# Attention, routed experts and a rational MLP on one core: decay rows, first transfers, gates and the attention order changed

## The chip, the core and the metric

The kernel runs on one core of a Trainium2 chip. Five engines work side by side, each through its own list of instructions in order: TensorE (PE, its weight loads shown as PEld), VectorE (DVE), ScalarE (ACT), GpSimd (POOL) and SyncE (SP, which here only issues transfers). They wait for each other and for transfers by semaphores. The metric is device time in microseconds (us), less is better.

## The reference

Three stages, in fp32. Attention with a decay, per batch b (4) and head h (8), S = 576, D = 64:

```python
scores = q @ k.T / sqrt(D);  cum = cumsum(log(clip(f, 1e-4, 1)))
scores = where(causal, -1e9, scores + cum[:, None] - cum[None, :])
attn = softmax(scores);  x = attn @ v          # x: (2304, 512) after the heads are joined
```

Experts (8, one per token), on the 2304 tokens:

```python
logits = x @ w_gate;  e = argmax(logits);  gate_w = softmax(logits)[e]
eom = sigmoid((x @ w_output_gate)[e])
out = gate_w * eom * (relu(x @ w1[e]) @ w2[e])  # w1: 512x1024, w2: 1024x512
```

Then a dense pair 512 to 2048 to 512 with g = P(h)/Q(h) between, a cubic over a quadratic in |h|.

The gate of a token, gate_w * eom, is a positive number, so it may be put on the token's row of x ahead of the expert or on the expert's output.

## The kernel before, in words

**Attention.** Work goes by pairs of heads: 16 pairs, four to a batch. A pair's scores are made in seven steps of 128 query rows (L456 and its neighbours: one product with the high parts of k and q, kh and qs, and one with kl and q2s). kl holds the low part of k and, in two more rows, the pair's decay (high and low part), q2s a copy of q and two rows of ones, so that one product adds the low part and the decay. DVE takes the row minimum (L478, L490; the scale is negative), ACT the exponential (L510, L521), PE transposes (L573, L593), DVE or ACT copies the result to SBUF (L290, L292: pT), PE multiplies by v (L616: po), and DVE or ACT copies to ot. The splits into high and low parts are made per half pair: kh (L410) on DVE, qs (L421) on ACT, the low parts and q2s (L415, L424, L429) on POOL, for pair 0 on DVE.

The decay rows come from one chain at the start: load f, clip, log on ACT, a running sum on DVE (L314, scan), its high part (L328) and low part (L332), two stores to DRAM (cum_d), and for every pair a load of two rows for each head into kl (L387).

**Order.** The attention part's order is written by a planner: each operation has a `when` (a priority from constants T_... times the pair's number), a modelled length on each engine that may do it, and the operations and buffers that it needs; of what is ready at about the same time the one with the least `when` goes first, and a copy that two engines could do goes to the one with the earlier modelled end plus DEAR. What comes out is the order on each engine, SP's transfers included.

**Batches.** When the four pairs of a batch are done, DVE inverts the sums (rc, L691), PE and DVE make the logits (L699 to L724), choose (L739 to L744) marks each token's expert in oh, and the gates follow: gates_a on DVE (L750 to L752), gates_x on ACT (L755, L756), gates_b on DVE (L760 to L769), whose last two operations multiply rc by the gate: rg. Then the batch's rows are transposed (L779), scaled by rg (on DVE for batches 0 and 1, L785; copied by ACT and scaled on POOL for 2 and 3) and stored to x_d, five tiles a batch.

**Tail.** After the last pair DVE's order is fixed by hand: choose of batch 3, then a count of the tokens before each token (two matmuls with onesb and after, a scan, cnt, nsl, send, base), interleaved with gates_b; from it a slot of 128 tokens and a place for each token (pos, sidx, pp), one-hot products (so, rs, op_) and a matmul whose result is ids, the token of each place. POOL gathers the rows by ids.

**Experts.** 22 slots: transpose the gathered rows, split into high and low, first matrix (L1169 to L1171), relu, transpose, second matrix, copy (ys, L1193), store to y_d. The expert's weights are split by split_unit (high on ACT, low on DVE, L1037). slot_info makes the list by which weights are loaded. Beside it the dense weights are decoded in pieces (loads from POOL's queue, L1203).

```python
DEAR = {"ACT": 45.9, "DVE": 316.0}      # L37
o_z = plan.op(early, {"DVE": 600}, f_zero, takes=["pr"])
o_f = plan.op(early, {"SP": 1900}, f_load, takes=["t"])
l_c = plan.op(tl + 0.3 * SPAN, {"SP": 1200}, load_c, o_cst, takes=["c"])
for i in range(NI):
    rows_out(i)                          # behind gates_b and the count
nc.scalar.activation(ys, yp.pop(s), AF.Copy)   # L1193
```

Of the kernel before, what the change touches and what calls it, by code (L numbers as in the profile page):

```python
# [21 lines left out]
P = 128  # L22
# [15 lines left out]
DEAR = {"ACT": 45.9, "DVE": 316.0}  # L38

NEAR = 108.2  # L40
# [6 lines left out]
class Op:  # L47
# [90 lines left out]
def tile_attention_moe_mlp(  # L138
# [44 lines left out]
    cum_d = dram.tile([NBH, 2, S], F32, name="cum_d")  # L183
    x_d = dram.tile([NT, DM], F32, name="x_d")
    y_d = dram.tile([NSLOT * P, DM], F32, name="y_d")
# [4 lines left out]
    identf = const.tile([P, P], F32, name="identf")  # L190
    make_identity(nc, identf)

    after = ec.tile([P, P], BF16, name="after")
    nc.gpsimd.memset(after, 1.0)
# [4 lines left out]
    onesb = ec.tile([P, P], BF16, name="onesb")  # L199
    nc.gpsimd.memset(onesb, 1.0)  # L200
# [11 lines left out]
    pref = ec.tile([P, NE], F32, name="pref")  # L212
    nc.gpsimd.iota(pref, pattern=[[-1, NE]], base=NE, channel_multiplier=0, allow_small_or_imprecise_dtypes=True)

    prefs = ec.tile([P, NI, NE], F32, name="prefs")
    nc.gpsimd.tensor_copy(prefs, pref.unsqueeze(1).to_broadcast([P, NI, NE]))
    nc.gpsimd.memset(prefs[TL:, NQ], 0.0)


    with ExitStack() as actx, ExitStack() as rctx:  # L220
# [30 lines left out]
        nc.gpsimd.memset(mask, 0.0)
        nc.gpsimd.memset(mask_t, 0.0)
        for t in [mask[:, (NQ - 1) * P :]] + [mask_t[h * TL : (h + 1) * TL, S // 2 - TL :] for h in range(2)]:
            nc.gpsimd.affine_select(
                out=t, in_=t, compare_op=ALU.is_ge, fill=BIG / SCALE, base=0, pattern=[[-1, t.shape[-1]]], channel_multiplier=1
            )

# [8 lines left out]
        T_STEP = (0.003, 0.167, 0.576, 1.046, 0.372, 0.855, 1.261)  # L266
        T_TRANS = (0.59, 0.851, 0.237, 0.235, -3.102, 0.47, -0.137)
        T_MOVE = (1.284, 1.144, 0.583, -2.797, 0.532, -7.775, 0.103)
        T_LEAST, T_EXP, T_SPLIT, T_SPLIT2 = 0.096, 0.218, 0.342, 0.209
        T_PV, T_PV2, T_OUT = -2.976, 4.84, -4.781  # L270
        T_BATCH, T_BATCHJ, T_ROWS = 0.299, 0.239, -5.772
# [22 lines left out]
        def evac_len(n):  # L294
            return {"ACT": 60 + 0.836 * n, "DVE": 85 + 1.04 * n}

# [29 lines left out]
        def f_high(e):  # L326
            g0["ch"] = wt("pr")[:NBH].bitcast(F32R)
            nc.scalar.activation(g0["ch"], g0["cum"], AF.Copy, scale=1.0 / SCALE)  # L328

        def f_low(e):  # L330
            g0["cl"] = wt("pr")[:NBH].bitcast(F32R)
            nc.vector.scalar_tensor_tensor(  # L332
                g0["cl"], g0["cum"], 1.0 / SCALE, g0["ch"].bitcast(F32), ALU.mult, ALU.subtract
            )

        def f_store(i, t):
            return lambda e: nc.sync.dma_start(out=cum_d[:, i, :], in_=g0[t].bitcast(F32))
# [1172 lines left out]
```

## Time and profile before

| what | value |
|---|---|
| median of 3 runs | 916.08 us (915.52 to 918.97) |
| profiled execution: its own time, its span | 916.76 us, 915.0 us |
| busy share: PE, PEld, DVE, ACT, POOL | 95%, 79%, 81%, 68%, 37% |
| chain that ended last, by engine | PE 41%, DVE 1%, ACT 1% |
| most expensive PE groups | dense layers (L1378 to L1380, L1423 to L1425), experts (L1169 to L1171) |

Shares are means over stages that differ, so the rows below go by stretches: the start to about 30 us, attention to 193, the tail to 220, experts to 500, dense layers to 900. A row of the time order gives start, duration, engine, line, operation, what is written and read, the number merged, and in brackets how long the engine had stood idle and what released it.

### The profile page before, as it was taken

What the parts mean: (1) busy time and instruction counts of PE and PEld (TensorE: products, weight loads), DVE (VectorE), ACT (ScalarE), POOL (GpSimd) and SP (SyncE); (2) the same over time, 40 slices, a digit from 0 to 9 for tenths busy, and PEclk for the clock granted to TensorE, in tenths of its full rate; (3) what the DMA queues carried; (4) which work ended last, traced back from release to release, by engine and by line L of the source; (5) the groups of instructions that cost most, each with busy time, mean ns of one, the idle gap of its engine ahead of it and who ended that gap; (6) DMA issues with size and microseconds to landing.
All of it is one profiled execution on the core that took longest, in us unless ns stands there. A gap on an engine that the chain in (4) does not pass through costs nothing. (4 is left out here: it accounts for less than half of the span.)

```text
span 915.0 us, 14857 instructions
## 1 busy us (share of the span) xinstructions
PE 868.4 (95%) x4733; PEld 720.1 (79%) x4733; DVE 742.2 (81%) x1395; ACT 619.1 (68%) x1261; POOL 339.6 (37%) x356
## 2 busy tenths in 40 slices
PE   6999998976799999999999999999999999999996
PEld 5787786754688888788887778889888889988885
DVE  7798999778676689788864899989898888989873
ACT  4889887773364567666643787877676667777664
POOL 7788595534212213223121124243332324324223
PEclk9999999997999999999999999999999999999999
DMA  6675567415755378878743312011000001000001
GB/s 173 153 203 159 159 183 209 144 53 179 253 179 196 103 265 290 294 255 300 238 150 108 124 61 66 1 47 27 20 35 13 24 0 47 24 1 35 1 1 46
DMA packets 50147, 110.25 MB, mean 120 GB/s; under 512 B 8405, under 2 KB 12526, under 8 KB 50062
## 3 DMA queue, kind: packets, MB, share of 16 engines
q1 hardware_dynamic: 39214, 74.09, 26.4%
q0 software_dynamic: 10848, 35.14, 11.3%
q8 instruction: 39, 0.64, 0.3%
q14 instruction: 46, 0.38, 0.1%
HBM read 151.79 MB, written 20.35 MB: 188 GB/s over the span
## 5 line engine op out<-in xcount | busy, mean ns | idle before, releaser
L1409 POOL TENSOR_TENSOR gl<-raw,gh 128x512 fp32r<-128x512 f32 (+1 forms) x80 | 95.8, 1199 | 242.7 <-ACT gh L1408 150.2
L1425 PE MATMUL pa<-wu,gl 128*128 128x512 f32 x288 | 113.0, 392 | 1.1 <-POOL gl L1409 1.1
L1423 PE MATMUL pa<-wu,gh 128*128 128x512 f32 x288 | 113.7, 395 | 0.0
L1424 PE MATMUL pa<-wu,gh 128*128 128x512 f32 x288 | 112.6, 391 | 0.0
L1388 ACT ACTIVATE raw<-ph 128x512 f32<-128x512 f32 (+1 forms) x80 | 44.3, 553 | 80.1 <-PE ph L1380 76.8
L1064 DVE TENSOR_TENSOR colAl<-px,colAh 128x512 fp32r<-128x512 f32 x70 | 47.9, 687 | 48.7 <-ACTq L1075 25.3
L1037 DVE TENSOR_TENSOR wu<-raw,wu 128x1024 fp32r<-128x1024 f32 x64 | 75.4, 1221 | 8.4 <-ACT wu L1035 8.0
L510 ACT ACTIVATE pr<-t,mn 128x384 f32<-128x384 f32 (+3 forms) x128 | 70.6, 555 | 16.1 <-DVE mn L478 15.6
L1391 DVE SCALAR_TENSOR_TENSOR raw<-raw,babs 128x512 f32<-128x512 f32 (+1 forms) x80 | 60.8, 761 | 24.3 <-ACT raw L1389 23.8
L1401 DVE SCALAR_TENSOR_TENSOR raw<-raw,coef,raw 128x512 f32<-128x512 f32 (+1 forms) x80 | 66.0, 825 | 17.4 <-ACT raw L1397 14.4
L1378 PE MATMUL ph<-colAh,wi 128*128 128x512 f32 x192 | 74.9, 390 | 0.8 <-ACTq L1319 0.8
L1379 PE MATMUL ph<-colAl,wi 128*128 128x512 f32 x192 | 74.8, 390 | 0.2 <-DVEq L1319 0.2
L1380 PE MATMUL ph<-colAh,wi 128*128 128x512 f32 x192 | 74.7, 389 | 0.0
L1169 PE MATMUL ph<-wu,colAh 128*128 128x512 f32 x176 | 73.8, 420 | 0.7 <-ACT colAh L1063 0.7
L1169 PE MATMUL py<-wu,colAh 128*128 128x512 f32 x176 | 70.9, 403 | 1.3 <-ACT colAh L1063 1.3
L1171 PE MATMUL ph<-wu,colAl 128*128 128x512 f32 x176 | 69.8, 396 | 0.0
L1170 PE MATMUL ph<-wu,colAh 128*128 128x512 f32 x176 | 69.6, 396 | 0.0
L1171 PE MATMUL py<-wu,colAl 128*128 128x512 f32 x176 | 69.0, 392 | 0.2 <-DVE colAl L1064 0.2
L1170 PE MATMUL py<-wu,colAh 128*128 128x512 f32 x176 | 68.7, 391 | 0.0
L1063 ACT ACTIVATE colAh<-px 128x512 fp32r<-128x512 f32 x70 | 41.6, 596 | 37.4 <-PE px L1184 26.1
L1035 ACT ACTIVATE wu<-raw 128x1024 fp32r<-128x1024 f32 x64 | 63.8, 1053 | 3.2 <-DMA raw<-in_w_dram 2.8
L1425 PEld LDWEIGHTS pa<-wu,gl 128*128 128x128 f32 x288 | 54.0, 188 | 14.0 <-POOL gl L1409 2.4
(236 smaller groups left out, 2428.7 us busy)
## 6 DMA issues: line engine op xcount, KB each, us to landing
raw<-in_w_dram SPq DMA_DIRECT2D x92, 1024.0 KB
rk<-in_kT_dram SPq DMA_DIRECT2D x30, 288.0 KB
rq<-in_qT_dram SPq DMA_DIRECT2D x30, 288.0 KB
d<-in_w_in_dram POOLq DMA_DIRECT2D x16, 512.0 KB, 3.9
d<-in_w_out_dram POOLq DMA_DIRECT2D x16, 512.0 KB, 5.6
y_d<-ys SPq DMA_DIRECT2D x22, 256.0 KB
v<-in_v_dram SPq DMA_DIRECT2D x16, 256.0 KB
wo_d<-d SPq DMA_DIRECT2D x16, 256.0 KB
```

Source lines behind the costliest of these rows:

```text
L510: nc.scalar.activation(u["pr"][:, sl], u["t"][:, sl], AF.Exp, bias=u["mn"][:, m : m + 1], scale=-1.0, accum_out=sm[:, i, 2 * hp + h : 2 * ...
L1037: nc.vector.tensor_tensor(w[:, 1], r, w[:, 0].bitcast(F32), ALU.subtract)
L1169: nc.tensor.matmul(ps, hi[:, c, :], w[:, 0, c, :], start=start and c == 0, stop=False)
L1170: nc.tensor.matmul(ps, hi[:, c, :], w[:, 1, c, :], start=False, stop=False)
L1171: nc.tensor.matmul(ps, lo[:, c, :], w[:, 0, c, :], start=False, stop=stop and c == KD - 1)
L1378: nc.tensor.matmul(out_, wh, hi[:, :, c], start=(c == 0), stop=False)
L1379: nc.tensor.matmul(out_, wh, lo[:, :, c], start=False, stop=False)
L1380: nc.tensor.matmul(out_, wl_, hi[:, :, c], start=False, stop=(c == KD - 1))
L1409: nc.gpsimd.tensor_tensor(d["gl"], d["u_"], d["gh"].bitcast(F32), ALU.subtract)
L1423: nc.tensor.matmul(a_, gh[:, sl], wh, start=(m == 0), stop=False)
L1424: nc.tensor.matmul(a_, gh[:, sl], wl_, start=False, stop=False)
L1425: nc.tensor.matmul(a_, gl[:, sl], wh, start=False, stop=(m == MF - 1))
```

## The change

1. The decay's high and low parts are written to a tile in SBUF (cc, in raw[3]) and copied from there into kl; cum_d and its two stores are gone. raw[3]'s weight load now waits for the last such copy.
2. At the start ACT's queue issues pair 0's rq and its decay copy, SP's the rest. POOL's constants stand in another order; pair 0's low parts may go to POOL or DVE; coef is loaded during attention.
3. Rows of x are scaled by rc alone. The gates are stored to gate_d, gathered by ids for each slot, and scale ys. In the tail the rows come ahead of choose and gates_b behind ids. Batches 0 and 1 store x_d from SP.
4. The count works in units of 128 tokens, with fewer operations (ahead in place of base; onesb and after hold 1/128).
5. The planner's constants are new; a batch's rows have their own times (T_ROWS, T_ROWJ), batch 2's included.
6. The first slot is transposed ahead of the second weight split.

```diff
-DEAR = {"ACT": 45.9, "DVE": 316.0}
-NEAR = 108.2
+DEAR = {"ACT": -28.382, "DVE": 213.971}
+NEAR = 48.171
...
-        lat = 1000 if self.engine == "SP" else LATENCY.get((self.engine, engine), 200)
+        lat = 2000 if self.engine in ("SP", "AQ") else LATENCY.get((self.engine, engine), 200)
...
-        T_BATCH, T_BATCHJ, T_ROWS = 0.299, 0.239, -5.772
+        T_BATCH, T_BATCHJ, T_ROWS = -0.09391, 0.42965, -0.41658
+        T_ROWJ = 1.3601
...
         def f_high(e):
-            g0["ch"] = wt("pr")[:NBH].bitcast(F32R)
-            nc.scalar.activation(g0["ch"], g0["cum"], AF.Copy, scale=1.0 / SCALE)
+            nc.scalar.activation(cc[:, 0], g0["cum"], AF.Copy, scale=1.0 / SCALE)
...
-                    nc.sync.dma_start(out=kls[p % 2][r : r + 2, h, :].bitcast(F32), in_=cum_d[2 * p + h])
+                    queue[e].dma_start(
+                        out=kls[p % 2][r : r + 2, h, :].bitcast(F32), in_=cc[2 * p + h : 2 * p + h + 1].bitcast(F32)
+                    )
...
-                q_ = plan.op(tl, {"SP": n}, load("rq", qT, h0, h1), takes=["rq"] if h0 == 0 else [])
+                q_ = plan.op(tl, {"SP" if p else "AQ": n}, load("rq", qT, h0, h1), takes=["rq"] if h0 == 0 else [])
...
-                for r in ((slice(0, P), slice(0, NQ)), (slice(0, TL), slice(NQ, NI))):
-                    nc.vector.tensor_tensor(
-                        g["rg"][r[0], r[1], :], g["rc"][r[0], r[1], :],
...
+            def gates_d(e=None):
+                r = gate_d[b * S : (b + 1) * S]
+                nc.sync.dma_start(out=r[: NQ * P].rearrange("(i p) o -> p (i o)", p=P), in_=g["den"][:, :NQ])
+                nc.sync.dma_start(out=r[NQ * P :], in_=g["den"][:TL, NQ:])
...
-                    g["rg"][:np_, i].unsqueeze(2).to_broadcast([np_, H, D]), ALU.mult,
+                    g["rc"][:np_, i].unsqueeze(2).to_broadcast([np_, H, D]), ALU.mult,
...
-                    plan.op(w, {"POOL": 1100}, lambda e, i=i, y=y: rows_d(i, y, nc.gpsimd), [o_m], frees=[("xr", o_m)])
+                    plan.op(w, {"SP": 1500}, lambda e, i=i, y=y: rows_d(i, y, nc.sync), [o_m], frees=[("xr", o_m)])
...
-        for i in range(3):
+        for i in range(NI):
             rows_copy(i)
+            rows_out(i)
         vector_order = rctx.enter_context(tc.manual_schedule(engines={mybir.EngineType.DVE}))
         choose()
...
+        nc.vector.tensor_scalar(cnt, cnt, HALF, ROUND, op0=ALU.add, op1=ALU.add)
+        nc.vector.scalar_tensor_tensor(nsl, cnt, ROUND, few, ALU.subtract, ALU.max)
...
+        nc.vector.scalar_tensor_tensor(ahead, cume[:, 0:NE], HALF, send0[:, 0:NE], ALU.add, ALU.subtract)
...
         nc.vector.tensor_scalar_add(ids, pid[:, :NSLOT], float(NT // 2))
+        gates_b()
+        gates_d()
...
+        def gather_gate(s):
+            gather_word(gate[:, s : s + 1], gate_d[:, :], ids[:, s : s + 1])
...
-                nc.scalar.activation(ys, yp.pop(s), AF.Copy)
+                nc.scalar.activation(ys, yp.pop(s), AF.Identity, scale=gate[:, s : s + 1])
...
         split_unit(0, hi=False)
+        trans_x(0, col_of(0))
         split_unit(1, hi=False)
-        trans_x(0, col_of(0))
```

DVE at the start, before (t and pr are the tiles of the decay chain, rk and rq the loads of pair 0):

```order
L306 MEMSET pr 32x576
L321 TENSOR_SCALAR t<-t 32x576
L314 SCALAR_TENSOR_TENSOR t<-pr 32x576
L410 CAST kh<-rk 128x576
L415 TENSOR_TENSOR kl_119<-rk,kh 64x576
L332 SCALAR_TENSOR_TENSOR pr<-t,pr 32x576
L424 TENSOR_TENSOR qs_113<-rq,qs_113 64x576
L429 TENSOR_SCALAR q2s_117<-rq 64x576
L410 CAST kh<-rk 128x576
L415 TENSOR_TENSOR kl_119<-rk,kh 64x576
L429 TENSOR_SCALAR q2s_117<-rq 64x576
L424 TENSOR_TENSOR qs_113<-rq,qs_113 64x576
```

DVE at the start, now:

```order
L244 MEMSET kl_108 128x1152
L318 MEMSET pr 32x576
L435 TENSOR_SCALAR q2s_106<-rq 64x576
L333 TENSOR_SCALAR t<-t 32x576
L430 TENSOR_TENSOR qs_104<-rq,qs_104 64x576
L435 TENSOR_SCALAR q2s_106<-rq 64x576
L326 SCALAR_TENSOR_TENSOR t<-pr 32x576
L416 CAST kh<-rk 128x576
L421 TENSOR_TENSOR kl_108<-rk,kh 64x576
L342 SCALAR_TENSOR_TENSOR raw_81<-t,raw_81 32x576
L416 CAST kh<-rk 128x576
L421 TENSOR_TENSOR kl_108<-rk,kh 64x576
L416 CAST kh<-rk 128x576 x2
```

The two q2s copies and the low part of q stand ahead of the scan (the row pr to t) now, kh and kl behind it, and pair 1's kh ahead of the first minimum.

DVE at the gates of batch 1 (den, rg), before:

```order
L752 TENSOR_REDUCE oz<-gs 128x5
L292 COPY ot<-po 128x320
L410 CAST kh<-rk 128x576
L760 TENSOR_REDUCE den<-ex 128x5
L762 TENSOR_SCALAR den<-den 128x5
L764 SCALAR_TENSOR_TENSOR den<-oz,den 128x5
L766 RECIPROCAL den<-den 128x5
L769 TENSOR_TENSOR rg<-rc,den 128x32
L769 TENSOR_TENSOR rg<-rc,den 64x8
L478 ISA t,mn<-s,mask 128x384
```

The same gates now, in pair 14 instead of pair 12:

```order
L301 COPY ot<-po 128x320
L301 COPY ot<-po 128x256
L301 COPY pT<-pt 128x4x64
L767 TENSOR_REDUCE den<-ex 128x5
L768 TENSOR_SCALAR den<-den 128x5
L769 SCALAR_TENSOR_TENSOR den<-oz,den 128x5
L770 RECIPROCAL den<-den 128x5
L485 ISA t,mn<-s,mask 128x384
```

The rows of rg are gone, and no kh stands just ahead.

DVE in the tail behind cnt, before:

```order
L760 TENSOR_REDUCE den<-ex 128x5
L918 TENSOR_SCALAR quot<-cnt 128x8
L919 TENSOR_SCALAR nsl<-quot 128x8
L762 TENSOR_SCALAR den<-den 128x5
L958 TENSOR_SCALAR nsl<-nsl 128x1
L764 SCALAR_TENSOR_TENSOR den<-oz,den 128x5
L960 SCALAR_TENSOR_TENSOR send_3241<-nsl,zero 128x8
L766 RECIPROCAL den<-den 128x5
L964 TENSOR_TENSOR base<-send_3241,nsl 128x8
L769 TENSOR_TENSOR rg<-rc,den 128x32
L966 SCALAR_TENSOR_TENSOR base<-base,cume 128x8
L769 TENSOR_TENSOR rg<-rc,den 64x8
```

DVE in the tail from cnt on, now:

```order
L956 TENSOR_TENSOR cnt<-cume 128x8
L957 TENSOR_SCALAR cnt<-cnt 128x8
L958 SCALAR_TENSOR_TENSOR nsl<-cnt,few 128x8
L959 SCALAR_TENSOR_TENSOR send_3242<-nsl,zero 128x8
L962 SCALAR_TENSOR_TENSOR ahead<-cume,send_3242 128x8
L963 TENSOR_TENSOR pos_3239<-pos_3239,ahead 128x160
L964 TENSOR_TENSOR pos_3239<-pos_3239,oh 128x160
L966 TENSOR_REDUCE pos<-pos_3239 128x20
L970 TENSOR_SCALAR sidx<-pos 128x20
```

The rows of den and rg have left; of the count four rows stand ahead of the position sum.

## Rows read from the trace of the kernel before

**Rows 1.** Table of stretches: us, busy time (count) by engine, PEclk, DMA share, GB/s.
```profile
30.00:193.00 163.00, 153.98 (x1272) 125.33 (x1272) 145.16 (x491) 137.74 (x434) 108.47 (x107) 1.00 0.58 159
...
193.00:220.00 27.00, 13.43 (x99) 7.94 (x99) 21.90 (x53) 14.97 (x24) 15.68 (x14) 0.75 0.31 103
...
220.00:500.00 280.00, 274.55 (x1323) 224.82 (x1324) 205.93 (x294) 156.35 (x238) 63.91 (x73) 0.99 0.66 224
...
510.00:897.00 387.00, 385.86 (x1805) 328.53 (x1804) 341.37 (x501) 284.46 (x513) 120.68 (x104) 1.00 0.08 27
```

**Rows 2.** Instructions in order of time, 0 to 22 us: start, us, engine, line, operation.
```profile
3.94 1.34 DVE L314 TENSOR_TENSOR_SCAN t<-pr 32x576 f32<-32x576 f32 x1 [0.75 <-ACT pr L310]
...
6.40 1.10 SPq L373 DMA_DIRECT2D rq<-in_qT_dram  x2
...
8.05 1.32 DVE L429 TENSOR_SCALAR q2s<-rq 64x576 fp32r<-64x576 f32 x1
...
9.75 0.68 ACT L421 ACTIVATE qs<-rq 128x576 fp32r<-128x576 f32 x1 [2.92 <-DMA rq<-in_qT_dram]
...
12.03 0.58 SPq L387 DMA_DIRECT2D kl<-cum_d  x2
...
13.52 0.41 PE L456 MATMUL s<-kl,q2s 128*128 128x384 f32 x1 [4.19 <-DMA kl<-cum_d]
```

**Rows 3.** Table of stretches, start of the attention part.
```profile
5.00:6.00 1.00, 1.00 (x13) 1.00 (x11) 0.90 (x3) 0.68 (x1) 0.94 (x2) 1.00 0.94 256
...
24.00:28.00 4.00, 3.73 (x16) 2.77 (x16) 2.07 (x6) 2.80 (x11) 2.41 (x3) 0.57 1.02 242
```

**Rows 4.** Instructions in order of time, 20 to 34 us.
```profile
21.43 1.26 ACT L421 ACTIVATE qs<-rq 128x576 fp32r<-128x576 f32 x2 [1.39 <-DMA rq<-in_qT_dram]
...
23.23 0.20 PEld L593 LDWEIGHTS pt<-identf,pr 128*128 128x128 f32 x2 [2.99 <-ACT pr L510]
```

**Rows 5.** Waits of PE, 30 to 190 us: in total, times, longest.
```profile
PE s L466 <- DVE mn L478: 4.8, 2, 2.6
```

**Rows 6.** DVE in order of time, 134 to 148 us.
```profile
140.97 1.39 DVE L762 TENSOR_SCALAR den<-den 128x5 f32<-128x5 f32 x1
...
142.47 1.36 DVE L764 SCALAR_TENSOR_TENSOR den<-oz,den 128x5 f32<-128x5 f32 x1
```

**Rows 7.** POOL in order of time, the same stretch.
```profile
140.91 1.42 POOL L415 TENSOR_TENSOR kl<-rk,kh 64x576 fp32r<-64x576 f32 x1 [3.53 <-DVE kh L410]
```

**Rows 8.** DVE in order of time, 88 to 103 us.
```profile
98.33 1.31 DVE L769 TENSOR_TENSOR rg<-rc,den 128x32 f32<-128x32 f32 x2
```

**Rows 9.** Groups by shape, DVE, 30 to 193 us: busy, mean ns, idle before.
```profile
L292 DVE COPY pT<-pt 128x256 f32<-128x256 f32 x12 | 4.9, 413 | 0.4 <-PE pt L573 0.4
```

**Rows 10.** Instructions in order of time, 190 to 240 us.
```profile
198.25 0.20 DVE L739 TENSOR_REDUCE lmax<-lgb 128x5 f32<-128x40 f32 x1
...
200.01 1.04 PE L779 MATMUL pt<-identf,ot 128*128 128x128 f32 x8
...
202.63 0.20 DVE L760 TENSOR_REDUCE den<-ex 128x5 f32<-128x40 f32 x1 [1.12 <-ACT ex L755]
...
204.04 3.28 POOL L785 TENSOR_TENSOR pr<-pr,rg 128x512 f32<-128x512 f32 x3 [1.42 <-DVE rg L769]
...
204.37 1.05 DVE L979 TENSOR_TENSOR pos<-pos,oh 128x160 f32<-128x160 f32 x1
...
209.28 0.67 DVE L991 TENSOR_TENSOR so<-s,sidx 128x500 f16<-128x500 f16 x1
...
214.00 0.19 DVE L1007 TENSOR_SCALAR ids<-pid 128x25 int32<-128x25 f32 x1 [0.40 <-PE pid L1005]
...
214.31 4.63 DVE L1037 TENSOR_TENSOR wu<-raw,wu 128x1024 fp32r<-128x1024 f32 x4
...
220.18 0.50 PE L1169 MATMUL ph<-wu,colAh 128*128 128x512 f32 x1 [0.69 <-ACT colAh L1063]
```

**Rows 11.** Groups by shape, POOL, 214 to 520 us: busy, mean ns, idle before.
```profile
L1150 POOL DMA_INDIRECT dtok<-sid_d,yrow x18 | 19.4, 1078 | 5.5 <-issue 3.7 <-DVE wu L1037 1.2 <-DVE colAl L1064 0.3
```

More of the change, by code (lines that the diff above doesn't have):

```diff
@@ L187, in tile_attention_moe_mlp @@
     sid_d = dram.tile([NSLOT * P, 1], I32, name="sid_d")
-    identf = const.tile([P, P], F32, name="identf")
-    make_identity(nc, identf)
+    onesb = ec.tile([P, P], BF16, name="onesb")
+    nc.gpsimd.memset(onesb, 1.0 / P)
     after = ec.tile([P, P], BF16, name="after")
-    nc.gpsimd.memset(after, 1.0)
+    nc.gpsimd.memset(after, 1.0 / P)
     nc.gpsimd.affine_select(
@@ L256, in tile_attention_moe_mlp @@
             )
+        for t in qs:
+            nc.gpsimd.memset(t.bitcast(F32)[:, :, S:], 0.0)
+        make_identity(nc, identf)
+        nc.gpsimd.memset(kls[1].bitcast(F32), 0.0)
+        blank(1)
+        for t in vs:
+            nc.gpsimd.memset(t[: P - TL, :, NQ], 0.0)
+        pref = ec.tile([P, NE], F32, name="pref")
+        nc.gpsimd.iota(pref, pattern=[[-1, NE]], base=NE, channel_multiplier=0, allow_small_or_imprecise_dtypes=True)
+        prefs = ec.tile([P, NI, NE], F32, name="prefs")
+        nc.gpsimd.tensor_copy(prefs, pref.unsqueeze(1).to_broadcast([P, NI, NE]))
+        nc.gpsimd.memset(prefs[TL:, NQ], 0.0)
         CUT = NQ // 2
@@ L295, in evac_len @@
             return {"ACT": 60 + 0.836 * n, "DVE": 85 + 1.04 * n}
+        queue = {"SP": nc.sync, "AQ": nc.scalar}
         g0 = {}
@@ L807, in batch @@
             if b == B - 1:
-                return choose, gates_a, gates_x, gates_b, rows_t, rows_m, rows_c, rows_g, rows_d
-            late = b == B - 2
+                return choose, gates_a, gates_x, gates_b, gates_d, rows_t, rows_c, rows_g, rows_d
             o = plan.op(wn(), {"DVE": 1000}, choose, prev_red)
@@ L852, in tile_attention_moe_mlp, with load_coef @@
         plan.op(SPAN, {"SP": 1300}, load_wl, [st[0]["o_ot"]])
+        coef = const.tile([P, 6], F32, name="coef")
+        def load_coef(e):
+            nc.sync.dma_start(out=coef[:, 0:4], in_=ca.to_broadcast([P, 4]))
+            nc.sync.dma_start(out=coef[:, 4:6], in_=cb.to_broadcast([P, 2]))
+        plan.op(3 * SPAN, {"SP": 1300}, load_coef, [st[1]["o_ot"]])
+        plan.op(early, {"POOL": 6000}, lambda e: None)
         with tc.manual_schedule():
             plan.emit()
-        choose, gates_a, gates_x, gates_b, rows_t, rows_m, rows_c, rows_g, rows_d = last_of
+        choose, gates_a, gates_x, gates_b, gates_d, rows_t, rows_c, rows_g, rows_d = last_of
         last_y = [{} for _ in range(NI)]
@@ L867, in rows_out @@
             rows_d(i, last_y[i], nc.sync)
-        coef = const.tile([P, 6], F32, name="coef")
-        nc.sync.dma_start(out=coef[:, 0:4], in_=ca.to_broadcast([P, 4]))
-        nc.sync.dma_start(out=coef[:, 4:6], in_=cb.to_broadcast([P, 2]))
         neg = const.tile([P, 4], F32, name="neg")
@@ L933, in tile_attention_moe_mlp @@
         gates_x()
-        for i in range(3, NI):
-            rows_copy(i)
         incl, pos3 = t_(SH, name="incl"), t_(SH, name="pos3")
@@ L969, in tile_attention_moe_mlp @@
-        counting = count()
-        for _ in range(3):
-            next(counting)
-        for _ in gates_b():
-            next(counting, None)
-        for _ in counting:
-            pass
-        for i in range(NI):
-            rows_out(i)
-        nc.vector.tensor_tensor(pos3, pos3, base.unsqueeze(2).to_broadcast(SH), ALU.add)
+        ahead = const.tile([P, NE], F32, name="ahead")
+        HALF = (P - 1) / (2.0 * P)
+        nc.vector.tensor_tensor_scan(
+            out=incl.rearrange("p e c -> p (e c)"), data0=ptot[:, :NEC], data1=zero, initial=0.0,
+            op0=ALU.add, op1=ALU.add,
+        )
@@ L1136, in slot_tokens @@
             nc.sync.dma_start(out=sid_d.rearrange("(s p) o -> s (p o)", p=P), in_=idr)
+        gate = const.tile([P, NSLOT], F32, name="gate")
         order0 = 0
@@ L1239, in slot_alone @@
             gather(s)
+            gather_gate(s)
             for u in range(4):
```

164 lines of the change are left out of this document (63 added, 101 removed).

## Prediction

> **What bounds the kernel now.** I read the table of stretches first, then the chain of waits at the start, the waits inside the attention part, and the tail between attention and the experts. [rows 1] gives the stages: experts (220 to 500) and dense layers (510 to 897) keep PE busy 274.6 of 280 and 385.9 of 387 us, and the change leaves their matmuls as they are. So a gain has to come from the other three places: the start, the attention part (PE 154.0 of 163 us, DVE 145.2: 9.0 us of PE idle, a second engine close behind) and the tail (PE 13.4 of 27).
>
> At the start PE's first product with the decay rows waits 4.19 us for their load and runs at 13.52 [rows 2]. At 21.43 ACT has stood 1.39 us for pair 1's q, and PE, behind the exponentials queued after it, 2.80 us [rows 4]; and from 24 to 28, after that pause, the granted clock is 0.57 on average, most of it at the 1.2 GHz level [rows 3]. Inside attention PE has two long waits for DVE's row minimum, 4.8 us in all [rows 5]. Both lie where DVE does the gates of a batch: two operations on five numbers a row take 1.39 and 1.36 us [rows 6], exactly as long as POOL's two low-part operations that run then [rows 7]; the scaling of rg takes 1.31 [rows 8]. In the tail DVE's chain sets the end: choose from 198.25, ids at 214.00, first expert matmul at 220.18 [rows 10].
>
> **Start.** SP no longer carries rq of pair 0, the two stores of the decay rows, the constants ahead of them and the store's round trip. Added: rq and the decay load on ACT's queue, and a new order on DVE. There the second q2s copy, which waits for the last rq half, now stands ahead of the scan; behind the scan stand kh, kl and the low decay row, and for that waits ACT's load, then PE. Price: an rq half took 3.35 us from first issue to use, two issues 1.10 [rows 2]. ACT issues four after its table load (about 2.1), so until about 4.3. By then 1.25 MB are queued; at the 256 GB/s of [rows 3] they take 4.9 us from about 2.3, and part of v comes between: landed about 8.6. Then q2s (about 1.0; 1.32 in the trace), scan 1.34, kh and kl (1.25, which hide ACT's high row), the low row 0.74, and a load of 1.49 (13.52 less 12.03): 14.4, 0.9 later than before. Bounds: landing 2.25 us after the last issue ends, nothing in between, gives 11.9 (1.6 earlier); landing at 9.4 with everything slow 16.6 (3.1 later). I take +0.9.
>
> The other side: pair 1's k and q no longer stand behind the decay load at 12.03 [rows 2] but are issued from about 6 on, so ACT's 1.39 goes. What is late next is POOL, which still has constants and pair 1's low parts in a row; pair 1's first scores then come about 2.4 us earlier relative to pair 0, of PE's pause of 2.80 (bounds 0 and 2.8). The lower clock behind the pause cost 4 x 0.43 = 1.7 us [rows 3]; half of that is 0.9. Start: +0.9 - 2.4 - 0.9 = -2.4, bounds -6 and +3.
>
> The Trainium skill, page "DMA: Bandwidth & Descriptors", section "Issuing engines are not separate DMA queues", says that transfers issued from several engines share the same DMA engines, so a second issuer saves only the time to issue. The busy share of 0.94 at 5 to 6 us [rows 3] agrees. By that rule the second queue would bring nothing; it is my second rival.
>
> **Attention.** Removed: rg (two DVE operations a batch) and the rows' wait for the gates; ten x_d transfers leave POOL's queue for SP's. Moved: batch 2's rows from the tail into pairs 12 to 15, which is 20 transposes at 0.13 (1.04 for 8 [rows 10]) = 2.6 us of PE in a stretch where it is 94% busy: +2.2, bounds 0 and 2.6. Their ACT copies and POOL products lie beside PE. The gates: batch 0's stand again directly behind a kh cast, where POOL starts its low parts, but without rg: of the first wait 0.9 goes. Batch 1's now stand between pair 13's output copies and pair 15's first minimum, some 20 rows after the last kh, where POOL has finished: the second wait, 2.6, goes. Together -3.5, bounds 0 and -4.8. Evacuations: by form, DVE gets 15 of 256 columns at 0.413 [rows 9] and a few others, 7.9 us, against 2.2 of rg gone: +5.7 us in a stretch where it idles 17.8 [rows 1]. That idle time hides them; what it costs if the cover is gone is the third rival. ACT loses about as much. I price the rest of the new order at nothing, since no row shows whether it packs better: bounds -5 and +5. SP's added x_d transfers stand ahead of q loads that wait for buffers anyway; without that cover a load is late once, like the 1.39 of [rows 4]. Attention: 2.2 - 3.5 = -1.3, bounds -8 and +8 without the third rival.
>
> **Tail.** On DVE between cnt and the position sum stood twelve operations with a wait of 1.12 us for the gates' exponentials [rows 10]; now four. 1.12 + 0.5 = 1.6 us go. From 204.37 to 209.28 seven small operations took 4.91 us, beside POOL's products from 204.04 (3.28 for three) [rows 10]: a product of 160 columns took 1.05 where its like needs about 0.3. The products now need only rc and are issued before choose, so they end about 201; five operations remain at 0.2 to 0.35, about 1.2 us: 3.7 go. What is late next: choose itself now lies beside POOL. Its three products of two tiles in SBUF may each wait for a POOL product of 1.09: bounds 0 and +2.2, taken at +1.1. Batch 2's gates, four operations at 0.20 with two short exponentials on ACT, move ahead of the last normalisation: +0.4. Tail: -1.6 - 3.7 + 1.1 + 0.4 = -3.8, bounds -6 and -1.5.
>
> The Trainium skill, page "SBUF — State Buffer", section "Who interferes with whom", says that a VectorE operation with two SBUF inputs waits for a GpSimd operation that reads SBUF, and a reduction never. The trace agrees with the first half [rows 6, 10]; that choose's reductions stay free no row here shows. Taken literally the three products would cost the full +2.2 and the sum would be 910.0 instead of 908.9, within the forecast's own range.
>
> **Experts.** The second weight split (two of the four operations in 4.63 us [rows 10]) moves behind the first transposed tile, so slot_info is 2.3 us later. PE needs the split only after twelve matmuls and four transposes, about 3.5 us: covered by half a microsecond; if not, 2.3. Gate gathers: 22 on POOL at 1.08 [rows 11] in a stage where it is busy 63.9 of 280 us [rows 1]; each is issued about a slot (12.7 us) ahead of its use. They hold up the decode loads behind them by as much. The scaled copy replaces a plain one. +0.3, bounds 0 and +2.4.
>
> **Sum.** -2.4 - 1.3 - 3.8 + 0.3 = -7.2 us from the profiled execution's 916.76 (span 915.0): 909.6. The median of the runs is 0.7 lower, so 908.9.
>
> **Rivals.** (1) The attention order also packs better: the 9.0 us of PE idle go, less 2.6 of transposes, -6.4 instead of -1.3: -12.3, 903.8. For it: PE's waits there are DVE's and ACT's queue order, which the change rewrites. Against: DVE gets more work.
> (2) The start gains nothing: the engines' rate decides, both queues share it, the scan waits for the last q half, and pair 1 is late by POOL instead of by its load. +1.7 there instead of -2.4: -3.1, 913.0. For it: [rows 3] and the DVE order; against: the 1.39 wait that an earlier issue surely removes.
> (3) Slower: DVE becomes the pace of attention. Its idle time is 17.8 us over some 15 pairs, 1.2 a pair, and 5.7 more fall into some of them; there PE's scores wait for DVE's minimum to free a bank, 2.4 us each as in the two places of [rows 5]. If six more pairs do so and the gates' gain stays out: +14.4 + 2.2 in attention, 10.7 in all, 926.8. From two such places on the sum is above the time before. Against: ACT loses what DVE gets, and the removed rg ran in just these pairs.
>
> **How the numbers follow.** Forecast 0.45, own range 905 to 912.5; rival (1) 0.21, (2) 0.23, (3) 0.08; 0.03 for others. A difference under 0.5% of the 916.1 can't be told from none, so faster means below 911.5 and slower above 920.7. Faster: 0.45 x 0.85 + 0.21 + 0.23 x 0.2 = 0.64. Same: 0.45 x 0.15 + 0.23 x 0.75 + 0.03 = 0.27. Slower 0.09. The range 901 to 916 leaves out rival (3) and the far end of (1).
>
> **What would show it.** Start: PE's first product with kl at 14 to 15, and no wait of PE above 1 us between 20 and 26. Attention: a wait on the row minimum at batch 0's gates only, DVE busy some 150 us. Tail: from choose to ids about 12 us instead of 15.8, no operation of 20 columns above 0.3 us, POOL done before the count. Experts: PE without a wait behind its first twelve matmuls. Wrong if PE's idle time in attention grows, if the first kl product comes after 16.6, or if ACT waits for a gate.

## The result, and the profile after

The changed kernel takes 929.9 us in the median (925.6 to 934.6, 4 runs) against 917.1 before (915.5 to 919.0, run beside it): 1.0131 times as long, 95% interval 1.0097 to 1.0165. I had forecast 908.9 us, with a range up to 916. The profiled execution took 929.8 us, its span 928.1.

Where the 13.0 us of span lie is best read by milestones, taken from the instructions in order of time of each kernel (us from the span's start). "Pair n x v" is the start of the n-th pair's product with v. The last three columns are experiments told below.

| milestone | before | changed | e2 | e6 | e14 |
|---|---|---|---|---|---|
| first product with kl | 13.52 | 15.00 | 14.27 | 15.03 | 15.05 |
| pair 1 x v | 41.85 | 39.43 | 38.90 | 39.45 | 40.06 |
| pair 2 x v | 52.30 | 49.15 | 48.64 | 49.01 | 49.54 |
| pair 15 x v | 189.95 | 195.48 | 190.21 | 190.67 | 188.11 |
| ids | 214.00 | 215.97 | 210.72 | 211.18 | 208.61 |
| first tokens on PE | 218.83 | 229.88 | 216.22 | 216.68 | 213.27 |
| end of span | 915.0 | 928.1 | 914.2 | 914.2 | 912.3 |

Changed less before, stage by stage: to pair 1 x v -2.4; pair 1 to pair 15 148.1 to 156.05, +7.95; pair 15 to ids 24.05 to 20.49, -3.6; ids to the first tokens 4.83 to 13.91, +9.1; from there to the end +2.0. They add up to +13.0. So start and tail gained what was forecast, and two other places lost 17 us.

The tail of the changed kernel in order of time, which answers to [rows 10] (start, duration, engine, line, operation; in brackets the idle time before it and its releaser):

```profile
203.76 0.20 DVE L747 TENSOR_REDUCE lmax<-lgb 128x5 f32<-128x40 f32 x1
203.99 2.62 DVE L749 TENSOR_TENSOR sc<-lgb,lmax 128x40 f32<-128x40 f32 x1
...
206.64 0.20 DVE L750 TENSOR_TENSOR sc<-sc,prefs 128x40 f32<-128x40 f32 x1
...
215.97 0.18 DVE L991 TENSOR_SCALAR ids<-pid 128x25 int32<-128x25 f32 x1 [0.40 <-PE pid L989]
...
216.45 1.11 POOL L1134 DMA_INDIRECT xg<-x_d,ids  x1 [9.43 <-DVE den L767]
...
217.00 0.37 SPq L774 DMA_DIRECT2D gate_d<-den  x1
217.42 0.51 SPq L775 DMA_DIRECT2D gate_d<-den  x1
...
229.88 1.11 PE L1156 MATMUL px<-identf,xg 128*128 128x128 f32 x4 [9.68 <-DMA xg<-x_d,ids]
...
231.74 0.79 PE L1162 MATMUL ph<-wu,colAh 128*128 128x512 f32 x1 [0.75 <-ACT colAh L1049]
```

Choose to ids is 12.2 us where it was 15.75. Then the first gather of tokens, issued at 216.45, feeds PE only at 229.88: 13.4 us. Between them SP has issued the last batch's gates. In the kernel before, the same two rows lie 4.35 us apart:

```profile
214.48 2.00 POOL L1144 DMA_INDIRECT xg<-x_d,ids  x1 [4.70 <-DVE ids L1007]
...
218.83 0.66 PE L1163 MATMUL px<-identf,xg 128*128 128x128 f32 x4 [0.60 <-DMA xg<-x_d,ids]
```

The changed kernel's stretch in the table of stretches (busy times, then granted clock, DMA share, GB/s):

```profile
205.00:210.00 5.00, 0.43 (x2) 0.10 (x1) 4.58 (x16) 2.18 (x4) 2.01 (x3) 0.74 0.31 14
210.00:215.00 5.00, 0.73 (x14) 0.54 (x15) 4.83 (x11) 5.00 (x7) 0.00 (x0) 0.50 0.38 137
215.00:220.00 5.00, 4.35 (x19) 1.56 (x19) 3.75 (x8) 0.94 (x1) 2.94 (x3) 0.50 0.75 21
220.00:225.00 5.00, 0.20 (x1) 0.00 (x0) 0.00 (x0) 0.00 (x0) 0.28 (x1) 0.50 0.95 26
225.00:230.00 5.00, 0.12 (x1) 0.12 (x2) 0.00 (x0) 0.00 (x0) 0.00 (x0) 0.50 0.38 76
230.00:235.00 5.00, 4.25 (x12) 3.18 (x13) 3.24 (x5) 0.60 (x1) 3.42 (x4) 0.53 0.27 87
```

From 220 to 225 the DMA engines are busy 0.95 of the time and move 26 GB/s, while every engine stands. The queues from 215 to 231 us (packets, MB, share of 16 engines' time) show what fills it:

```profile
q0 software_dynamic: 240, 0.79, 66.0%
q1 hardware_dynamic: 608, 0.00, 1.8%
```

q1 is SP's queue: its 608 packets of 4 bytes, 576 of them words of the gates, take 1.8%, and 528 have begun by 219.0. q0 is GpSimd's: the gathers' packets take 66%, the longest of them 10.4 us, where none of the first gather's passes 0.7 us in the kernel before. So the words themselves are short, and the gather beside and behind them is slow; by what they hold it, no view shows.

PE's clock is still at the lower level when it starts, so its first products take 0.63 us instead of 0.40.

In the attention, PE's waits (24 to 196 us; in total, times, longest) answer to [rows 5]:

```profile
PE pt L600 <- DVE pT L301: 6.2, 4, 2.4
PE pt L600 <- DVE xr L787: 2.1, 1, 2.1
PE s L462 <- POOL qs L430: 1.6, 1, 1.6
PE pt L600 <- DVE sums L697: 0.8, 1, 0.8
```

The two waits for the row minimum are gone, as forecast; others have come, most of them for DVE. One of them, in order of time:

```profile
60.68 1.54 POOL L842 DMA_DIRECT2D y_d<-qs  x2
...
61.39 2.60 DVE L416 CAST kh<-rk 128x576 fp32r<-128x576 f32 x1
...
62.23 1.43 POOL L421 TENSOR_TENSOR kl<-rk,kh 64x576 fp32r<-64x576 f32 x1
...
63.91 0.48 DVE L301 COPY ot<-po 128x320 f32<-128x320 f32 x1
...
65.08 0.55 DVE L301 COPY pT<-pt 128x256 f32<-128x256 f32 x2
...
65.78 0.63 PE L600 MATMUL pt<-identf,pr 128*128 128x128 f32 x4 [2.37 <-DVE pT L301]
```

A copy of k's high part (kh) needs 0.45 us when nothing holds it; this one takes 2.60. GpSimd is issuing transfers when it starts and makes a low part (L421) inside it, and PE waits 2.37 us at the end of the queue behind it. Other held copies are simpler. This one ends 0.3 us behind the operation of GpSimd that it met:

```profile
116.44 1.41 POOL L421 TENSOR_TENSOR kl<-rk,kh 64x576 fp32r<-64x576 f32 x1 [1.06 <-DVE kh L416]
...
116.69 1.48 DVE L416 CAST kh<-rk 128x576 fp32r<-128x576 f32 x1
```

All 32 copies, min/median/max ns, changed and before:

```profile
L416 DVE CAST kh<-rk x32: 440/538/2601, 11.1 to 173.0; 128x576 fp32r<-128x576 f32 x32
```

```profile
L410 DVE CAST kh<-rk x32: 445/454/2255, 5.2 to 166.6; 128x576 fp32r<-128x576 f32 x32
```

From 28 to 190 us their mean is 942 ns against 653; 13 of those that begin there take more than 0.6 us, 7 before.

At the start, two rows answer to [rows 2, 4]: the first product with kl, and PE's pause, 1.56 us instead of 2.80.

```profile
15.00 0.66 PE L463 MATMUL s<-kl,q2s 128*128 128x384 f32 x1 [2.88 <-DMA kl<-raw]
...
24.02 0.44 PE L462 MATMUL s<-kh,qs 128*128 128x384 f32 x1 [1.56 <-POOL qs L430]
```

### The profile page after: what moved, and what is told of

It reads as the page before. It is cut to its first block, busy times and chain, and to the rows that moved or that the text cites. A ratio compares the mean times of both kernels' runs of the same rounds, so it can differ in the third digit from the quotient of the medians.

```text
span 928.1 us, 14889 instructions
## 1 busy us (share of the span) xinstructions
PE 869.1 (94%) x4732; PEld 720.8 (78%) x4733; DVE 752.6 (81%) x1403; ACT 615.6 (66%) x1241; POOL 357.3 (38%) x370
## 5 line engine op out<-in xcount | busy, mean ns | idle before, releaser
L517 ACT ACTIVATE pr<-t,mn 128x384 f32<-128x384 f32 (+3 forms) x128 | 70.5, 555 | 19.6 <-DVE mn L485 19.0
L1396 DVE SCALAR_TENSOR_TENSOR raw<-raw,coef,raw 128x512 f32<-128x512 f32 (+1 forms) x80 | 65.8, 822 | 17.6 <-ACT raw L1392 14.5
```

Of the source, the lines that this page charges most:

```text
L517: nc.scalar.activation(u["pr"][:, sl], u["t"][:, sl], AF.Exp, bias=u["mn"][:, m : m + 1], scale=-1.0, accum_out=sm[:, i, 2 * hp + h : 2 * ...
```

## Experiments

Two theories at first. **W**: the gates' stores, 576 elements of 4 bytes, hold the DMA engines while the first gather waits among them. **O**: the planner's new numbers order the attention badly. Ratios are to the kernel before, timed on the same chip.

### e1: without the stores of gates

```diff
             def gates_d(e=None):
-                r = gate_d[b * S : (b + 1) * S]
-                nc.sync.dma_start(...)      # two stores from den
+                pass
...
+            nc.sync.dma_start(out=gate_d.rearrange("(c p) o -> c (p o)", p=P), in_=even)   # even = identf[:NTILE]
```

> The changed kernel without the four batches' stores of gates; the table of gates is filled once, early, by 18 rows of 512 B (zeros and ones instead of gates: the scaling of the experts' outputs is left out, everything else stands). Theory W (words): the last batch's gates go out as 576 elements of 4 bytes right behind the ids, and these hold the DMA engines while the first gather of tokens waits among them. Then the first gather lands about 4 us after its issue (12.7 in the changed kernel), the first expert product starts near 223 instead of 231.7, and the time is 919 to 922. Rival X: the gather is late because the stores of the rows, now all on SP behind each other, land late. Then it still takes 10 us or more, and the time is 928 to 931.

Measured: 917.6 us, ratio 1.0009 [0.9991, 1.0027]; the first gather feeds PE 3.4 us after its issue (212.48 to 215.91), the first product starts at 217.31. W's account, with a time 1.4 us below its range and a first product 6 us ahead of its mark; 4 of these 6 lie in the attention, where this execution was quicker (pair 15 x v at 191.49 instead of 195.48). Rival X falls.

### e2: the last batch's gates as rows

```diff
         gates_b()
-        gates_d()
+        gt = ps_r("gt")
+        nc.tensor.transpose(gt[:NI, :P], bt[B - 1]["den"], identf)
+        gr = t_([NI, P], name="gr")
+        nc.vector.tensor_copy(gr, gt[:NI, :P])
+        nc.sync.dma_start(...)      # gr[:NQ] to 4 runs of 512 B, gr[NQ] to one of 256 B
```

> The changed kernel; only the last batch's gates are turned by TensorE to 5 rows, copied by VectorE and stored as 5 long elements instead of 576 of 4 bytes. Theory W: as without the stores, the first gather lands in 4 to 5 us, first expert product near 223, time 920 to 923 (0.5 us for the turn and the copy at most). Rival X: no change, 928 to 931. If the gathers of gates matter (rival G), no change either.

Measured: 919.8 us, ratio 1.0022 [1.0004, 1.0040], against 1.0131 [1.0097, 1.0165] of the changed kernel: 10 us from the last batch's 576 words turned into five rows. In order of time:

```profile
211.20 1.11 POOL L1140 DMA_INDIRECT xg<-x_d,ids  x1 [9.45 <-DVE den L767]
212.50 0.27 SPq L998 DMA_DIRECT2D gate_d<-gr  x1
...
212.83 0.23 SPq L999 DMA_DIRECT2D gate_d<-gr  x1
...
216.22 0.78 PE L1162 MATMUL px<-identf,xg 128*128 128x128 f32 x4
...
217.75 0.49 PE L1168 MATMUL ph<-wu,colAh 128*128 128x512 f32 x1 [0.75 <-ACT colAh L1055]
```

The store stands in the same queue, 0.75 us later behind the ids for the turn and the copy, and the gather takes 5.0 us. Of the 10 us, 8.4 are the gather's. W holds as far as it says that the words delay the gather.

### e3: the old numbers in the changed kernel

```diff
-DEAR = {"ACT": -28.382, "DVE": 213.971}
+DEAR = {"ACT": 45.9, "DVE": 316.0}
...
-                w = TR + i * T_ROWJ * SPAN
+                w = (NPAIR + T_ROWS) * SPAN + i if b == B - 2 else wn()
```

> The changed kernel with the planner's numbers of the kernel before (DEAR, NEAR, all T_ numbers; rows of batches 0 and 1 due behind their gates, of batch 2 as before); the stores of gates stay. Theory O (order): the new numbers' order of the attention costs some 8 us against the old order; then the last pair's product with v starts at 186 to 190 (195.5 in the changed kernel, 190.0 before) and the time is 921 to 925. Rival S (structure): rows without gates and their evacuations on VectorE cost it whatever the numbers; then it starts at 193 to 197 and the time stays at 927 to 932.

Measured: 937.9 us, ratio 1.0224 [1.0192, 1.0256]; pair 15 x v at 205.87. Neither theory expected it: with the old numbers the changed structure is 8 us slower still (PE waits 6.0 us in one place for the copies of batch 2's rows). O falls in this form.

### e4: without the gathers of gates

```diff
-            gather_word(gate[:, s : s + 1], gate_d[:, :], ids[:, s : s + 1])
+            nc.gpsimd.memset(gate[:, s : s + 1], 0.5)
```

> The changed kernel with its stores of gates, but the 22 gathers of gates replaced by GpSimd's memset of one column each (the scaling by gates is left out). Theory W: the first gather still takes 11 to 13 us, first expert product at 230 to 232, time 927 to 930. Rival G: it is the gathers of single words, on GpSimd's queue, that delay tokens and weights: then 919 to 924.

Measured: 928.9 us, ratio 1.0109 [1.0069, 1.0149]; the first gather takes 12.4 us. Rival G falls: the 22 gathers of words cost nothing that shows.

### e5, e6: the split's place, and all gates as rows

```diff
         split_unit(0, hi=False)
-        trans_x(0, col_of(0))
         split_unit(1, hi=False)
+        trans_x(0, col_of(0))
```

> The kernel with the last batch's gates as rows (e2), and the weights' split back where the kernel before has it: both halves ahead of the first transposes. Theory P (place of the split): in e2 VectorE does the second half (2.35 us) between the low part of the first tokens and the slots' table, so that the next expert's weights are asked for 7.2 us after the first transposes, not 4.0 as before. Put back, the table is done about 2.5 us sooner behind the first transposes and the time is 1.5 to 2.5 us below e2's: 917 to 918.5. Rival: the weights come at the rate of the DMA engines whatever the start; then 919 to 921 as e2.

> e5, and the gates of all four batches kept in one tile, turned once behind the ids and stored as 20 rows; no stores of 4 bytes are left, also not those of batches 0 to 2 during the attention and the row stores. Theory W holds for these too if the 1728 words cost DMA time that the loads of q, k, v and the row stores then wait for: 914 to 917, 1 to 3 us below e5. Rival: the attention's loads have room for them; then e5's time within 1 us.

Measured: e5 917.7 us, ratio 1.0002 [0.9984, 1.0019]; e6 919.3, ratio 1.0037 [1.0019, 1.0056]. In e5 the slots' table is done 4.4 us behind the first transposes (e2: 6.5), as theory P says, but its ratio lies 0.2% under e2's with intervals that overlap: the place of the split is not settled by time. e6 shows no gain from the words of batches 0 to 2, so these are hidden; e6 serves as the base of what follows.

### e7: the new numbers alone; e8: the words alone

e7 is the kernel before with DEAR, NEAR and the T_ numbers replaced; e8 the kernel before with this:

```diff
         nc.vector.tensor_scalar_add(ids, pid[:, :NSLOT], float(NT // 2))
+        words = t_([P, NI], name="words")
+        nc.vector.tensor_scalar_add(words, pid[:, :NI], 0.0)
+        nc.sync.dma_start(out=word_d[: NQ * P].rearrange("(i p) o -> p (i o)", p=P), in_=words[:, :NQ])
+        nc.sync.dma_start(out=word_d[NQ * P :], in_=words[:TL, NQ:])
```

> The kernel before with nothing but the new numbers of the planner (DEAR, NEAR, T_ numbers, batch 2's rows due as the new numbers put them). Theory O: the new numbers' order is slow by itself: last product with v 4 to 8 us later than before (190), time 921 to 926. Rival S (the changed structure makes the attention late): time 915 to 920. After e3 (old numbers in the new structure: 937.9) a third: numbers fit only their own structure, then 925 to 945.

> The kernel before with one thing added: 576 words of 4 bytes, stored by SP in the form of the gates' store as soon as the ids are there (to a table that nobody reads; VectorE makes them in one more instruction of 0.2 us). Theory W: the first gather lands 8 to 10 us later, the first expert product starts near 229 to 231 instead of 220.2, time 925 to 929. Rival X (it needs the changed kernel's row stores on SP, too): 917 to 919.

Measured: e7 936.0 us, ratio 1.0204 [1.0179, 1.0230]. With e3 this is the third answer: either set of numbers fits its own structure only. The new numbers cost the old structure 2%, the old numbers the new structure 0.9% (1.0224 against 1.0131). e8 925.6 us, ratio 1.0091 [1.0067, 1.0115], 8.4 us for two stores of 2.25 KB in all:

```profile
217.44 0.37 SPq L1011 DMA_DIRECT2D word_d<-words  x1
217.63 2.00 POOL L1149 DMA_INDIRECT xg<-x_d,ids  x1 [4.70 <-DVE words L1010]
217.86 0.51 SPq L1012 DMA_DIRECT2D word_d<-words  x1
...
229.65 1.11 PE L1168 MATMUL px<-identf,xg 128*128 128x128 f32 x4 [8.88 <-DMA xg<-x_d,ids]
```

12.0 us from issue to PE, in a kernel whose row stores and order are the old ones. That the words cost the first gather 8 to 9 us is shown from both sides. That they do it by keeping the DMA engines busy with themselves is not: in e8's trace all of them have begun by 219.2, the gather's first packet begins at 220.3, and still one of its packets lasts 8.2 us.

### e9, e10: GpSimd's splits narrowed, in e6 and in the kernel before

The attention was left. Its stretch from pair 2 x v to pair 15 x v is 137.65 us before (140.5 in e8, whose attention is the same) and 146.3 in the changed kernel; with the changed order again 145.2 in e4, 144.3 in e5, 142.6 in e1, 141.6 in e2, 141.7 in e6. The table of stretches over it (us, busy time of PE, PEld, DVE, ACT and POOL, clock, DMA share, GB/s), before, changed and e6:

```profile
52.30:189.95 137.65, 129.35 (x1074) 104.23 (x1073) 123.72 (x413) 116.31 (x368) 91.20 (x90) 1.00 0.59 165
...
49.15:195.48 146.33, 135.07 (x1098) 108.19 (x1097) 130.43 (x415) 116.30 (x360) 88.62 (x84) 0.99 0.64 164
...
49.01:190.67 141.66, 132.79 (x1097) 106.77 (x1096) 127.90 (x415) 115.99 (x360) 89.23 (x84) 1.00 0.63 169
```

PE is idle 8.30, 11.26 and 8.87 us in it. So of e6's 4.0 us more than before, 3.4 are work of PE, which has 20 transposes of batch 2's rows more here and 4 others, and only 0.6 are waits. The changed kernel's own execution has 2.4 us more waits than e6 and 2.3 us more of PE's time for the same work. Most of these 2.3 are the granted clock, which fell to the lower level (1.2 GHz) behind a wait of 2.09 us and stayed there while PE worked through:

```profile
125.38:128.79 3.41, 3.41 (x18) 3.38 (x17) 2.19 (x8) 1.72 (x6) 1.40 (x1) 0.51 0.62 231
```

In e1, e2 and e6 the clock is 1.00 throughout the stretch; e4 and e5 have one such fall each, and e8 has two, with PE no longer idle than in the same order before (8.3 us). So the falls, with the waits, are why executions of one order differ. **C**: collisions of VectorE and GpSimd. **D**: VectorE's 16 evacuations more.

```diff
-                        kl_[half[h], h], d["rk"][half[h], h], d["kh"][half[h], h].bitcast(F32), ALU.subtract
+                        kl_[half[h], h, :few_], d["rk"][half[h], h, :few_], d["kh"][half[h], h, :few_].bitcast(F32), ALU.subtract
...
+            few_ = 16 if p >= 2 else S
```

> e6 in the same order, but GpSimd's three splits of every pair from the third on (low part of k, low part of q, scaled q) cover 16 columns instead of 576: the scores are not the reference's, nor the routing, so only the attention is compared, by the time from pair 2's product with v to pair 15's (141.7 us in e6, 146.3 in the changed kernel, 137.7 before). Theory C (contention): VectorE's copies of k (mean 822 ns in e6, 653 before) and small instructions are held while GpSimd works; then the copies fall to 400 to 600 ns and the stretch to 134 to 138 us. Theory D (VectorE simply has 16 evacuations more): the stretch stays at 140 to 143.

> The kernel before with the same cut of GpSimd's three splits (scores and routing not the reference's). If the contention is what the changed kernel has more of (theory C), the stretch from pair 2's to pair 15's product with v moves less here than in e9: 137.7 to some 135 to 137. If both lose as much, GpSimd costs both the same and C does not explain the difference.

Measured: the stretch is 132.0 us in e9 (from 48.94 to 180.97) and 131.2 in e10 (52.01 to 183.20); the copies of k take 463 and 460 ns in the mean. Busy times of PE, PEld, DVE, ACT and POOL over 137 us that hold the stretch, e9 and then e10:

```profile
47.00:184.00 137.00, 135.32 (x1144) 110.80 (x1146) 115.95 (x435) 118.86 (x369) 26.01 (x85) 1.00 0.69 180
```

```profile
50.00:187.00 137.00, 135.24 (x1133) 110.89 (x1131) 113.24 (x430) 120.03 (x379) 26.44 (x90) 0.99 0.63 171
```

Without GpSimd's splits PE is busy 135 of 137 us in both orders, DVE's evacuations included, so D falls. GpSimd costs the changed attention 9.6 us (e6 less e9) and the former one 6.5. But of PE's idle time the cut takes 7.2 us there (8.87 to 1.68) and 6.5 here (8.30 to 1.76), and the former stretch lost 6.5 us where C expected 0.7 to 2.7: both orders pay nearly the same for GpSimd as a whole, and by the sign named for e10 these two runs do not show that C makes the difference. Since the cut also ends GpSimd's own lateness, it does not say which collisions.

### e11: sixteen evacuations moved to ScalarE

```diff
-                o = plan.op(w, evac_len(n), lambda e: evac(e, dst(), src()), [need], frees=free)
+                o = plan.op(w, evac_len(n), lambda e: evac(turns(e), dst(), src()), [need], frees=free)
```

> e6 in the same order, with every fourth evacuation that the planner gave VectorE done by ScalarE instead: 16 of them, as many as VectorE had gained by the change. Theory D: the stretch falls from 141.7 to 137 to 139 us, TensorE's waits for VectorE's pT from 5 us to under 2, time 914 to 917. Theory C: it falls by under 1.5 us, time 917 to 920.

Measured: 917.8 us, ratio 1.0000 [0.9982, 1.0018], stretch 141.9 (e6: 141.7). No gain in the stretch; the waits for DVE's pT fall to 3.4 us and 2.9 for ACT's come in their place. D falls again. The total lies 0.4% under e6's ratio with intervals that just miss each other, and no milestone of the two profiles says why; e5, with the same attention order, stands at 1.0002, so it may be e6's ratio that lies high.

### e12, e13: a reduction in place of the copy of k

```diff
-                    nc.vector.tensor_copy(d["kh"][:, h], d["rk"][:, h])
+                    nc.vector.tensor_reduce(d["kh"][:, h], d["rk"][:, h].unsqueeze(2), AX.X, ALU.max)
```

> e6 in the same order, with the copy of k's high part made by VectorE's tensor_reduce over one element (same values, slower by itself: some 650 ns against 460 unhindered). The Trainium skill (SBUF, Who interferes with whom) says that tensor_reduce never contends with GpSimd where a copy in a two-port mode does. Theory C (the copies of k are held by GpSimd, and hold it): copies at 640 to 680 ns whatever GpSimd does (822 in e6), the stretch from pair 2's to pair 15's product with v 136 to 139 us (141.7 in e6), time 913 to 917. Rival H: the small instructions of the gates and sums beside GpSimd's work are what holds TensorE; then the stretch stays at 140 to 143 and the time at 918 to 921.

> The kernel before with the same tensor_reduce for k's high part. Its copies took 653 ns in the mean, little more than the reduce will, so theory C expects next to nothing: stretch 136 to 139 us (137.7), time 915 to 918. Rival: if the collision costs both kernels the same, it gains as much as e12 over e6, 2 to 5 us.

Measured: e12 914.1 us, ratio 0.9962 [0.9944, 0.9980], against 1.0037 [1.0019, 1.0056] of e6 and 1.0002 of e5: 4 to 7 us, by one instruction that is slower taken alone. Its 32 executions, min/median/max ns, in e12, and the copy's in e6:

```profile
L416 DVE TENSOR_REDUCE kh<-rk x32: 715/743/755, 11.1 to 166.1; 128x576 fp32r<-128x576 f32 x32
```

```profile
L416 DVE CAST kh<-rk x32: 442/520/1668, 11.1 to 168.2; 128x576 fp32r<-128x576 f32 x32
```

The copy spreads over a factor of four, the reduction over 40 ns, at more than the 640 to 680 expected. The Trainium skill, page "SBUF — State Buffer", section "Who interferes with whom", says that a copy or cast may run in a mode that takes the port pair shared with GpSimd and then waits for it, and that a reduction never does; these two rows agree with both halves. PE's waits in e12:

```profile
PE pt L780 <- DVE sums L689: 1.8, 1, 1.8
PE pt L600 <- DVE pT L301: 1.2, 1, 1.2
PE pt L600 <- DVE xr L786: 0.9, 1, 0.9
```

The waits for pT fall from 5.2 us in e6 to 1.2; the stretch is 138.6 us (141.7) and PE's idle time in it 5.6 (8.9). That is 3.1 us where the medians differ by 5; e6's profiled execution was its quickest. e13 takes 915.9 us, ratio 0.9995 [0.9972, 1.0017], its stretch 139.3 us, 0.3 above its range, with PE idle 8.4 us (8.3 before): no difference, as C expects, since there fewer copies were held and a reduction of 743 ns replaces a mean of 653.

### e14: the reduction from the second pair on

```diff
+                    if p:
                         nc.vector.tensor_reduce(d["kh"][:, h], d["rk"][:, h].unsqueeze(2), AX.X, ALU.max)
+                    else:
+                        nc.vector.tensor_copy(d["kh"][:, h], d["rk"][:, h])
```

> e12, but the first pair's two copies of k's high part are copies again (nothing runs beside them that holds them). The first low product starts at 15.0 us as in e6 instead of 16.25; if start and attention add, the time is 1 us below e12's: 912 to 914. Rival: the start's microsecond is taken up in the first pairs, then 913.5 to 915.

Measured: 914.1 us, ratio 0.9969 [0.9956, 0.9983]. The first product with kl is back at 15.05 from 16.25, and in the traces 0.8 of these 1.2 us are still there at the first tokens (213.27 from 214.09). The medians do not show it; intervals of 0.13% and more to either side cannot, so neither expectation is decided. e12 and e14 both beat both kernels, by 0.3 to 0.4% of the one before and by some 16 us of the changed one.

## Why the prediction was wrong

**Start, -2.4: right in sum, by luck.** Pair 1 x v came 2.42 us earlier, pair 2's 3.15. The first product with kl came at 15.00, not 14.4, and PE's pause kept 1.56 us that I had let go, behind POOL's low part of q. So pair 0 x v came 2.3 us later (29.72 against 27.39) where 0.9 was forecast, and from there to pair 1 x v it is 9.7 us instead of 14.5, 4.8 less where 3.3 were forecast: two misses that cancel. The clock was 1.00 from 24 to 28 us instead of 0.57, but 0.50 from 12.8 to 19.6, as long as the two lower stretches of before together (14.1 to 17.5 and 24.3 to 27.7), with PE busy 4.6 us in them instead of 6.7; what its 0.9 was worth is not shown. Rival (2) did not happen. (The lower bound of 11.9 for kl comes to 12.4 by the terms that it is given with.)

**Tail, -3.8: right in sum.** Measured -3.6. Choose's first product waited 2.4 us for POOL's rows, the other two did not wait at all (2.62, then 0.20 and 0.33 us); I had put +1.1, bound +2.2, and the other parts gained 6.0 us instead of 4.9. The reductions beside POOL stayed at 0.20.

**Experts, +0.3 with bounds 0 and +2.4: the first step that failed.** It counted the gates' gathers, the split and the scaled copy, and left out what gates_d itself issues: two stores whose elements are single words, right behind the ids that the first gather waits for. A DMA was priced at its issue and its bytes. It measured +9.1 us (e2 takes it away, e8 puts it into the kernel before). The gathers, which I did count, cost nothing (e4). Of the 2 us that the experts' stage lost besides, half-clock products behind the longer wait are one part (PE is busy 0.7 us longer); in e2, e5, e6, e11, e12 and e14, without that wait, the way from the first tokens to the end is still 697.6 to 699.7 us, with PE idle 16.7 to 17.7, against 696.2 and 15.3 before (694.8 and 14.2 in e13), and its cause stays open.

**Attention, -1.3: the second.** The gates' stalls went, as the step said, and the evacuations are hidden, as it said (e9, e11). The transposes, put at +2.2, cost about 3.4 (e6). What failed is the sentence that priced the rest of the new order at nothing. I had seen small operations stretched to the length of POOL's [rows 6, 7] and charged POOL's company to the gates alone; the copies of k, 32 of them against a handful of gates, stand in the same queue and were already at a mean of 653 ns where an unhindered one needs 454. In the new order more of them are held: 942 ns, 8 us of DVE. Between pair 0 x v and pair 15 x v PE stood idle 9.0 us before, 8.9 in e6 and 11.3 in the changed kernel; with the collision taken away by the kind of instruction alone it is 5.6 (e12), 3.4 us less than before, which is the gates' -3.5. So the held copies took that gain back, 3.3 us in e6 and 5.7 in the changed kernel's own execution. In the old order the same instruction changes nothing (9.0 us, e13). The last 2.3 us in the changed kernel are PE's own time, most of it the fall of the clock at 125.4. My rival (3) had the sign, DVE's lateness, but a wrong cause: it counted DVE's work, and there was enough room for that. What is not settled is why the same copy is held longer in one execution than in another (a mean of 822 ns in e6 and of 942 in the changed kernel, in one order).

The signs I had named read so: kl at 15.00 and choose to ids 12.2 held; "no PE wait above 1 us between 20 and 26" and "PE without a wait behind its first twelve expert matmuls" did not, and PE's idle time between pair 0 x v and pair 15 x v grew from 9.0 to 11.3 us, which the text had called a refutation.

## What to carry to other kernels

Price a store by its contiguous elements, not by its bytes, and look at what waits in the DMA engines just then: a column of one word per partition can be turned on TensorE first, for 0.7 us here (0.38 for the turn, 0.28 for the copy). When an order is changed, look for instructions whose duration spreads (min against max of one form) before counting busy time; a spread says that a neighbour holds them, and another form of the same instruction may be free of it. A planner's tuned numbers belong to one structure; test a change with numbers fitted to it, and neither set alone.

## What the runs showed of the hardware

576 stored words of 4 bytes, issued 0.55 us behind a gather, made it 9 us late: 13.4 us instead of 4.35 from its issue to its use (12.0 in e8), at a busy share of the DMA engines up to 0.95 and 21 to 26 GB/s. The words' own packets took 1.8% of the engines' time from 215 to 231 us, the gathers' 66%. The Trainium skill, page "DMA: Bandwidth & Descriptors", section "Rules for kernel authors", says that a last dimension that isn't contiguous becomes one descriptor per element and should be rearranged; e2 agrees: SP's 608 packets there become 10, for 10 us. Reads of single words by the gathers showed no such price (e4).

A copy on VectorE that meets an operation of GpSimd can be held until that has ended: 1.48 us instead of 0.45 beside one of 1.41, up to 2.60 where GpSimd issued transfers first. A reduction over one element in its place took 715 to 755 ns in all 32 cases (e12).
